# Forgetting attention and an MLP on one core: the shift as the exponential's bias, the start's decay rows re-cut, and unit 0's second layer in another order

## The chip, the core and the metric

The kernel runs on one core of a Trainium2 chip. A core has five engines with a queue each: PE (TensorE, matrix products), DVE (VectorE), ACT (ScalarE), POOL (GpSimd) and SP (SyncE, which here only issues DMAs). PE reads SBUF and writes PSUM; DVE and ACT read and write both; 16 DMA engines move data between HBM and SBUF. The metric is the device time of one execution in microseconds (us). The profile is one execution taken by the hardware profiler.

## The reference, cut to what matters

Inputs are q, k, v of shape (8 batches, 8 heads, 576 positions, 64) and f of shape (8, 8, 576), all float32, and two weights, 512 x 2048 and 2048 x 512.

```python
scores = scale * np.matmul(q, k.transpose(0, 1, 3, 2))          # scale = 1/8
log_f = np.log(np.clip(f, 0.0001, 1.0))
cum = np.cumsum(log_f, axis=-1)
decay = cum[:, :, :, None] - cum[:, :, None, :]
scores = np.where(causal, -1000000000.0, scores + decay)
attn = softmax(scores)                                          # written out, with + 1e-09 under the division
x = (attn @ v).transpose(0, 2, 1, 3).reshape(4608, 512)
h = x @ w_in
out = (h - np.tanh(h)) @ w_out
```

A term that is the same for all keys of one query leaves the softmax as it is: it multiplies numerator and denominator alike. The kernel uses this twice: a constant shift of 5 stands in place of the maximum, and the query's own decay need not be exact.

## The kernel before, in words

**Attention.** Work goes by pairs of heads, `pairs[p]` for p = 0 to 31, four pairs (`NPAIR`) in each of the eight batches. A score tile is computed transposed: keys on the partitions, queries along the columns. For one pair `TILES` lists seven score tiles (`ti` 0 to 6) of up to 512 columns. Each is a few matmuls into a PSUM tile `ps` (L358), one ACT exponential into an f16 tile `e` (or `el` for the tile of the last 64 keys, L367), and a causal mask: in batch 0 a matmul that adds -60000 through the tile `late` (L361), in the others a POOL select (L377). `values` multiplies `e` by `vn`, which holds v and a column of ones, into `av` (L395); DVE divides (L404 to L406) into `xn`; `turn` transposes `xn` into `XR`, the MLP's input, with PE and a copy in batch 0 (L423, L425, L427) and with two SP DMA transposes in the others (L429, L431).

**The decay inside the scores.** The matmul's contraction has 64 rows of the head and three more, kept in rows 64 to 66 of the tiles `QT` and `KT`. With the scale of 1/8 taken out, K's rows hold `chi` (8 cum, rounded to f16), `clo` (what the rounding left) and 1; q's rows hold -1, -1 and `cq` (8 cum - 40, f16). The product adds 8 (cum_q - cum_k) - 40 to 8 times the score, and the exponential's scale of 1/8 brings it back, with the shift of 5. The rows are moved into `QT` and `KT` by DMAs (`aug_rows`): on POOL for batch 0 (`bulk`, L219 to L221), on SP for the others (`load_aug`, L207).

**The first pair** does not wait for those DMAs. Its tiles are `QS` and `KS` (in the trace both are called W, since they lie in the weights' room), with 24 extra rows, three for each head of batch 0, at partitions 64 to 87 (`NH` to `NX`). `lf` holds f for 64 rows of all heads and again three times for batch 0's heads, so that `cum` has the values where they are wanted. For these rows `KS` gets -chi, 1 and the rest (L198), and q's row gets, for the head h in question alone, 1, 8 cum - 40 and -1 (`row_q`, L580, one ACT instruction for each head): q chooses the head. Per-partition factors for this lie in the columns of `per` (L179 to L191).

**The order.** All five engines run in the order in which the code issues (`manual_schedule`); nothing is reordered by a planner. At the start, DVE sets constants, clips f (L185), ACT takes Ln (L192) and loads the table for Exp (L193), DVE sums along the row (the scan, L195), makes chi (L197) and K's extra rows. `start` then issues pair 0: PE fills its time with matmuls on constants (`unread`, tile `idle`), transposes the raw q and k of the pair (L304), ACT copies q (L315), DVE copies k (L317) into `QS` and `KS` by head and half, and the first two score tiles follow. `bulk` issues the rest of batch 0's loads on POOL. From there `att_items(p)` gives the order within pair p: at given `ti` it puts the score tile, the transposes and copies of the next pair's q (`at_q`) and k (`at_k`), `values` of the pair before and `turn` of the one before that. The argument `copies` of `trans` names the engine of each copy, V for DVE and A for ACT.

**POOL's queue** issues the loads of q, k, v and the weights (they convert f32 to f16) in that same order, among the selects. `LOADS` says at which (p, ti); the first half of w_in is at (1, 0), the first of w_out at (4, 0).

**The MLP.** Its work goes by units of 512 tokens, woven into the attention from pair 4 on (`TAKE` is how many steps a pair gets). `mlp1` makes one of 16 blocks of 128 features: four matmuls into `hps` (L457), ACT's tanh into `th` (L462), DVE's sum into `gq` (L468). Features 0 to 7 are half 0 of `gq`, 8 to 15 are half 1. The second layer of unit 0 is `mlp2_plain`: 16 steps of eight matmuls each into `ops` (L498); four steps fill one PSUM bank, which holds two blocks of 128 tokens (`m`), each the sum over both halves of the features. The later units use `mlp2` (L523), which has seven products in place of eight.

Of the kernel before, what the change touches and what calls it, by code (L numbers as in the profile page):

```python
# [8 lines left out]
FP32 = mybir.dt.float32  # L9
FP16 = mybir.dt.float16  # L10
AF = mybir.ActivationFunctionType
# [5 lines left out]
SHIFT = 5.0  # L17
# [4 lines left out]
def kernel(  # L22
# [134 lines left out]
    nc.vector.memset(late, 0.0)  # L157
    nc.vector.memset(KT[0][:, :, S:PITCH], 0.0)
    chi = cst.tile([NX, S], FP16)
    clo = cst.tile([NH, S], FP16)  # L160
    cq = cst.tile([NH, S], FP16)
    KS = W1.rearrange("p k e -> p (k e)")[:, 0:2 * PITCH].rearrange("p (a n) -> p a n", a=2)
    QS = W2.rearrange("p k e -> p (k e)")[:, 0:2 * S].rearrange("p (a n) -> p a n", a=2)
    nc.vector.memset(KS[0:NX, :, S:PITCH], 0.0)
    per = cst.tile([NX, 9], FP32)
    nc.vector.memset(vn[0][D:P, NJ - 1, :, :], 0.0)
    isb, isc, mul_k, add_k, mul_l, mul_0, add_0, mul_1, add_1 = (per[:, i:i + 1] for i in range(9))
# [7 lines left out]
    def column(g, h):  # L175
        return id16[0:NX, NH + 3 * h + g:NH + 3 * h + g + 1]

    for to, g in ((isb, 1), (isc, 2)):
        nc.vector.tensor_reduce(out=to, in_=id16[0:NX, NH + g:NX:3], op=ALU.add, axis=mybir.AxisListType.X)  # L179
    nc.vector.tensor_scalar(out=mul_k, in0=isb, scalar1=-inv_qscale, scalar2=inv_qscale, op0=ALU.mult, op1=ALU.add)  # L180
    nc.vector.tensor_scalar_mul(out=add_k, in0=isb, scalar1=-1.0)
    nc.vector.tensor_scalar_mul(out=mul_l, in0=isc, scalar1=inv_qscale)
    for e in EL[0:2]:
        nc.vector.memset(e, 0.0)
    nc.vector.tensor_scalar(out=lf, in0=lf, scalar1=0.0001, scalar2=1.0,  # L185
                            op0=ALU.max, op1=ALU.min)
    nc.vector.memset(vn[0][:, :, :, D:VW], 1.0)
    for h, (mul, add) in enumerate(((mul_0, add_0), (mul_1, add_1))):
        nc.vector.tensor_scalar_mul(out=mul, in0=column(1, h), scalar1=inv_qscale)
        nc.vector.scalar_tensor_tensor(out=add, in0=mul, scalar=-SHIFT, in1=column(0, h), op0=ALU.mult, op1=ALU.add)  # L190
        nc.vector.tensor_tensor(out=add, in0=add, in1=column(2, h), op=ALU.subtract)  # L191
    nc.scalar.activation(out=lf, in_=lf, func=AF.Ln)  # L192
    nc.scalar.activation(out=expo, in_=lf[0:1, 0:1], func=AF.Exp)  # L193
    cum = TQ[0][0:NX, :, :].rearrange("p c s -> p (c s)").bitcast(FP32)[:, S:2 * S]
    nc.vector.tensor_tensor_scan(out=cum, data0=ones16, data1=lf, initial=0.0,  # L195
                                 op0=ALU.mult, op1=ALU.add)
    nc.vector.tensor_scalar(out=chi, in0=cum, scalar1=mul_k, scalar2=add_k, op0=ALU.mult, op1=ALU.add)  # L197
    nc.vector.scalar_tensor_tensor(out=KS[NH:NX, 0, 0:S], in0=cum[NH:NX, :], scalar=mul_l[NH:NX, :], in1=chi[NH:NX, :],  # L198
                                   op0=ALU.mult, op1=ALU.subtract)

    def aug_rows(b):
        i, hs = b % 2, slice(b * H, (b + 1) * H)
        return [(KT[i][D:D + 1, :, 0:S], chi[hs, :]), (KT[i][D + 1:D + 2, :, 0:S], clo[hs, :]), (QT[i][D + 2:D + 3, :, :], cq[hs, :])]

    def load_aug(b):
        for to, of in aug_rows(b):
# [6 lines left out]
    const_rows(0)  # L213

    def bulk():
        (k_hi, chi_0), (k_lo, clo_0), (q_hi, cq_0) = aug_rows(0)
        load_qk(qn, q, 0, 4, 6)
        load_qk(kn, k, 0, 4, 6)
        nc.gpsimd.dma_start(out=k_hi, in_=chi_0)  # L219
        nc.gpsimd.dma_start(out=q_hi, in_=cq_0)  # L220
        nc.gpsimd.dma_start(out=k_lo, in_=clo_0)  # L221
        load_qk(qn, q, 0, 6, H)
        load_qk(kn, k, 0, 6, H)
        for n in range(NJ - 1):
            load_v_block(0, n, 2, H)
# [117 lines left out]
    def scores(b, c, ti):  # L343
        if b == 0 and (((c - 1) * len(TILES) + ti) % 3 == 0 if c else ti == LAST):
            ps = ps_tr.tile([P, UW], FP32, tag="tr", name="ps")
        else:
            ps = ps_sc.tile([P, 512], FP32, tag="sc", name="ps")
        if ti == LAST:
            e = EL[(b * NPAIR + c) % 3]
        else:  # L350
            e = aex.tile([P, 512], FP16, tag="e", name="e")
        lo = min(x[4] for x in TILES[ti])
        hi = max(x[4] + x[3] for x in TILES[ti])
        kt, qt, rows = (KS, QS, NX) if b == 0 and c == 0 else (KT[b % 2], QT[b % 2], D + 3)
        for a, j, i0, n, col in TILES[ti]:
            h = 2 * c + a
            cut = min(P, n) if b == 0 and i0 == j * P else 0
            nc.tensor.matmul(out=ps[:, col:col + n], lhsT=kt[0:rows, h, j * P:(j + 1) * P],  # L358
                             rhs=qt[0:rows, h, i0:i0 + n], start=True, stop=cut == 0)
            if cut:  # L360
                nc.tensor.matmul(out=ps[:, col:col + cut], lhsT=id16, rhs=late[:, 0:cut],  # L361
                                 start=False, stop=True)
            for ib in range(j, NJ):
                w0 = min(ib * P, S - P)
                if i0 <= ib * P < i0 + n:
                    E[(b, c, a, j, ib)] = e[:, col + w0 - i0:col + w0 - i0 + P]
        nc.scalar.activation(out=e[:, lo:hi], in_=ps[:, lo:hi], func=AF.Exp, scale=qscale)  # L367
        if b == 0:
            return
        col, cp, step, wd = MASKS[ti]  # L370
        view = e[:, col:col + (cp - 1) * step + wd]
# [118 lines left out]
        nc.vector.tensor_tensor(out=LHS[name](u, i)[:, ks], in0=LHS[x](u, i)[:, ks], in1=LHS[y](u, i)[:, ks], op=op)  # L490

    def mlp2_plain(u, s):
        e, mp, m, half = s // 8, s // 4 % 2, s // 2 % 2, s % 2
        if s % 4 == 0:
            M2[u] = bank("ops").rearrange("p (m e) -> p m e", m=2)
        ops, t0 = M2[u], (2 * mp + m) * P
        for ft in range(half * NK, half * NK + NK):
            nc.tensor.matmul(out=ops[:, m, :], lhsT=GQ[(u, ft % NK // 4)][:, half, ft % 4, t0:t0 + P],  # L498
                             rhs=wout[:, ft, e * HE:(e + 1) * HE], start=(m == 0 and ft == 0),
                             stop=(m == 1 and ft == NFT - 1), skip_group_check=True)  # L500
# [75 lines left out]
    REST = []  # L576

    def start():
        def row_q(h, mul, add):
            nc.scalar.activation(out=QS[NH:NX, h, :], in_=cum[NH:NX, :], func=AF.Identity, bias=add[NH:NX, :], scale=mul[NH:NX, :])  # L580

        unread(47)
        row_q(0, mul_0, add_0)
        q_rest = trans(*pairs[0], qn, (QS,), True, "AAAA", True)
        nc.scalar.activation(out=cq, in_=cum[0:NH, :], func=AF.Copy, bias=-SHIFT * inv_qscale, scale=inv_qscale)
        unread(6)
        k_rest = trans(*pairs[0], kn, (KS,), True, "VVVV", True)
        unread(38)
        q_rest[0]()
        scores(*pairs[0], 0)  # L590
        unread(4)
        nc.vector.scalar_tensor_tensor(out=clo, in0=cum[0:NH, :], scalar=inv_qscale, in1=chi[0:NH, :], op0=ALU.mult, op1=ALU.subtract)
        nc.vector.tensor_copy(out=KS[NH:NX, 1, 0:S], in_=KS[NH:NX, 0, 0:S])
        for fn in k_rest:
            fn()
        scores(*pairs[0], 1)
        row_q(1, mul_1, add_1)
        unread(4)
        q_rest[1]()

    def last():
        nc.gpsimd.memset(KT[1][:, :, S:PITCH], 0.0)
# [4 lines left out]
    def att_items(p):  # L607
        def put(fn, *args):
            items.append((lambda: fn(*args), True))
# [6 lines left out]
        for ti in range(len(TILES)):  # L616
# [3 lines left out]
                items.append((lambda: const_rows(1), False))  # L620
                items.append((lambda: load_aug(1), False))
            if p == 0 and ti in (0, 2, 5, 6):
                put(unread, {0: 2, 2: 14, 5: 4, 6: 6}[ti])
            if p == 1 and ti == 6:
                put(unread, 8, True)
            if p == 1 and ti == 3:
# [100 lines left out]
```

## Time and profile before

| | us |
|---|---|
| median of 3 runs (341.08 to 341.85) | 341.27 |
| the profiled execution | 341.6 |
| its span | 339.9 |
| PE busy, of the span | 333.0 |
| DVE busy | 262.5 |
| ACT busy | 235.1 |
| POOL busy | 163.7 |
| first score of pair 0 | at 9.10 |
| first score of pair 1 | at 14.47 |
| first exponential of pair 2 | at 19.07 |
| first matmul of `mlp1` | at 28.91 |
| first matmul of `mlp2_plain` | at 50.75 |

Times inside the execution count from the start of the span. A row of the timeline reads: start, duration, engine, line, operation, output<-input, shapes, how many, and in brackets the idle time ahead of it and who ended it. PEld is PE's loading of the stationary operand, which overlaps its matmuls; rows with a q behind the engine's name (SPq) are DMAs being issued, and a transfer lands some microseconds later. A busy PE can be one that waits inside a group of matmuls, so the starts of the matmuls tell more than the share.

### The profile page before, as it was taken

The page shows a single profiled execution, that of the slowest core. Times are in us where ns is not written, and L with a number is a line of the kernel's source. Part 1 is how long each engine was busy: PE and PEld are TensorE (multiplying, and loading weights), DVE is VectorE, ACT ScalarE, POOL GpSimd, SP SyncE. Part 2 cuts the span into 40 slices and gives each one's busy share as a digit, 9 for nine tenths or more (in the row PEclk, how much of TensorE's full clock was granted, in tenths as well). Part 3 has the DMA queues.
Part 4 walks back from the last instruction along what each step waited for, and adds up shares of the span by engine and source line. Part 5 has one row for each costly group of instructions (what it writes and reads, how often), then busy time and mean ns, then how long its engine had stood idle before and what let it go on. Part 6 is the DMA issues. An engine that isn't in the chain of part 4 may idle for free.

```text
span 339.9 us, 8804 instructions
## 1 busy us (share of the span) xinstructions
PE 333.0 (98%) x3345; PEld 237.7 (70%) x3345; DVE 262.5 (77%) x516; ACT 235.1 (69%) x440; POOL 163.7 (48%) x323
## 2 busy tenths in 40 slices
PE   8999999999999999999999999999999999999995
PEld 8775557875588558855788888656875686486485
DVE  8898986659888888678967886688668766966864
ACT  6998777878987886778677867787558743632630
POOL 8894765885657573677377647632322210000000
PEclk9999999999999999999999999999999999999999
DMA  9999999999959999999999999990130023002003
GB/s 116 124 173 201 187 198 179 153 162 196 137 93 181 159 116 92 136 168 130 106 106 191 131 110 112 165 133 15 49 115 13 17 62 101 0 31 95 1 16 109
DMA packets 147535, 38.88 MB, mean 114 GB/s; under 512 B 128221, under 2 KB 146381, under 8 KB 147493
## 3 DMA queue, kind: packets, MB, share of 16 engines
q0 software_dynamic: 94592, 18.39, 74.1%
q1 hardware_dynamic: 52868, 19.88, 31.7%
q8 instruction: 26, 0.43, 0.5%
q14 instruction: 17, 0.13, 0.2%
q10 hardware_dynamic: 32, 0.06, 0.0%
HBM read 36.90 MB, written 9.44 MB: 136 GB/s over the span
## 4 chain that ended last, share of the span: by engine, by line
PE 85%; DVE 8%; DMA 2%; ACT 2%; issue 1%; ACTq 0%
PE hps L457 35%; PE ops L523 29%; PE ps L358 11%; PE av L395 7%; DMA XR<-xn 2%; PE ops L498 2%; DVE KT L317 2%; DVE QT L317 1%; ACT e L367 1%; DVE gq L468 1%; PE t L304 1%; DVE xn L406 1%; DVE W L317 1%; PE x L423 0%; DVE TQ L195 0%
## 5 line engine op out<-in xcount | busy, mean ns | idle before, releaser
L457 PE MATMUL hps<-XR,win 128*128 128x512 f16 (+1 forms) x640 | 140.9, 357 | 0.5 <-DMA XR<-xn 0.3
L462 ACT ACTIVATE th<-hps 128x512 f32<-128x512 f32 x144 | 86.6, 602 | 55.5 <-PE hps L457 52.8
L367 ACT ACTIVATE e<-ps 128x512 f16<-128x512 f32 x192 | 110.5, 598 | 9.8 <-PE ps L358 7.9
L468 DVE TENSOR_TENSOR gq<-hps,th 128x512 f16<-128x512 f32 x144 | 98.1, 687 | 24.2 <-ACT th L462 22.6
L377 POOL TENSOR_SCALAR_AFFINE_SELECT e<-e 128x128 f16<-128x128 f16 x168 | 60.3, 362 | 69.9 <-ACT e L367 67.9
L457 PEld LDWEIGHTS <-win 128*128 128x128 f16 x640 | 57.7, 97 | 48.7 <-issue 0.7
L358 PE MATMUL ps<-QT,KT 67*128 67x512 f16 (+1 forms) x372 | 73.8, 277 | 0.8 <-ACT e L367 0.4
L523 PEld LDWEIGHTS <-gq 128*128 128x128 f16 x640 | 60.2, 97 | 11.2
L523 PE MATMUL ops<-wout,gq 128*128 128x256 f16 x512 | 63.2, 272 | 0.0
L358 PEld LDWEIGHTS <-KT 67*128 67x128 f16 x372 | 35.3, 98 | 22.2 <-issue 1.2
L395 PEld LDWEIGHTS <-e 128*128 128x128 f16 x896 | 32.3, 97 | 3.6
L395 PE MATMUL av<-vn,e 128*128 128x65 f16 x896 | 33.6, 193 | 0.0
L131 POOL DMA_DIRECT2D vn<-in_v_dram x32 | 28.0, 878 | 7.5 <-DMA win<-in_moe_w_in_dram 3.4
L523 PE MATMUL ops<-W,sq 128*128 128x256 f16 x256 | 31.2, 272 | 0.0
L406 DVE TENSOR_TENSOR xn<-av,rs 128x640 f16<-128x640 f32 x32 | 26.4, 825 | 1.1
L523 PEld LDWEIGHTS <-sq 128*128 128x128 f16 x256 | 24.1, 97 | 3.4
L108 POOL DMA_DIRECT2D qn<-in_q_dram x25 | 21.1, 845 | 3.7 <-DMA wout<-in_moe_w_out_dram 1.9
L377 POOL TENSOR_SCALAR_AFFINE_SELECT el<-el 128x128 f16<-128x128 f16 x28 | 9.4, 337 | 26.9 <-ACT el L367 26.7
L108 POOL DMA_DIRECT2D kn<-in_k_dram x25 | 21.1, 845 | 1.5 <-issue 1.1
L404 DVE TENSOR_SCALAR rs<-av 128x10 f32<-128x10 f32 x32 | 5.2, 162 | 18.1 <-PE av L395 17.0
L498 PE MATMUL ops<-wout,gq 128*128 128x256 f16 x128 | 16.9, 272 | 0.4 <-DVE gq L468 0.3
L317 DVE COPY QT<-t 64x576 f16<-64x576 f16 x18 | 14.4, 801 | 3.5 <-PE t L304 3.4
(93 smaller groups left out, 321.0 us busy)
## 6 DMA issues: line engine op xcount, KB each, us to landing
out_dram<-ost SPq DMA_DIRECT2D x34, 256.0 KB
vn<-in_v_dram POOLq DMA_DIRECT2D x24, 128.0 KB, 5.6
qn<-in_q_dram POOLq DMA_DIRECT2D x20, 128.0 KB, 4.9
kn<-in_k_dram POOLq DMA_DIRECT2D x20, 128.0 KB, 5.0
win<-in_moe_w_in_dram POOLq DMA_DIRECT2D x2, 1024.0 KB, 12.3
wout<-in_moe_w_out_dram POOLq DMA_DIRECT2D x2, 1024.0 KB, 17.0
XR<-xn SPq DMA_TRANSPOSE x56
qn<-in_q_dram POOLq DMA_DIRECT2D x6, 144.0 KB, 4.7
```

Source lines behind the costliest of these rows:

```text
L108: nc.gpsimd.dma_start(out=dst[b % 2][0:pn, n, :].rearrange("p (h d) -> p h d", h=H), in_=src[b, :, n * P:n * P + pn, :].rearrange("h p d - ...
L131: nc.gpsimd.dma_start(out=vn[b % 2][:, n, h0:h1, 0:D], in_=v[b, h0:h1, n * P:(n + 1) * P, :].rearrange("h p d -> p h d"))
L317: nc.vector.tensor_copy(out=to, in_=of)
L358: nc.tensor.matmul(out=ps[:, col:col + n], lhsT=kt[0:rows, h, j * P:(j + 1) * P], rhs=qt[0:rows, h, i0:i0 + n], start=True, stop=cut == 0)
L367: nc.scalar.activation(out=e[:, lo:hi], in_=ps[:, lo:hi], func=AF.Exp, scale=qscale)
L377: nc.gpsimd.affine_select(out=view, in_=view, compare_op=ALU.is_ge, fill=0.0, base=0, pattern=pat, channel_multiplier=-1)
L395: nc.tensor.matmul(out=av[:, a, ib, :], lhsT=E.pop((b, c, a, j, ib)), rhs=vn[b % 2][:, j, 2 * c + a, 0:D + 1], start=(j == 0), stop=(j == ib))
L406: nc.vector.tensor_tensor(out=xn.rearrange("p i (a d) -> p a i d", a=2), in0=av[:, :, :, 0:D], in1=rs.to_broadcast([P, 2, NJ, D]), op=ALU. ...
L457: nc.tensor.matmul(out=hps[:, o:o + n], lhsT=win[:, ci, ft * P:(ft + 1) * P], rhs=XR[:, ci, t:t + n], start=(ci == 0), stop=(ci == NCH - 1))
L462: nc.scalar.activation(out=th, in_=hps, func=AF.Tanh, scale=-1.0)
L468: nc.vector.tensor_tensor(out=GQ[(u, i)][:, half, kt, :], in0=hps, in1=th, op=ALU.add)
L523: nc.tensor.matmul(out=ps[:, m, :], lhsT=LHS[lhs](u, kt // 4)[:, kt % 4, m * P:(m + 1) * P], rhs=rhs[:, kt, :], start=(fresh and (apart or ...
```

## The change

1. The shift of 5 is no longer part of the decay rows. A tile `shift` of 128x1 holds -5 and is the exponential's bias.
2. With that, q's decay row is 8 cum, which is chi; `cq` and its ACT instruction (L585) go, and `aug_rows` sends chi to q as well as to k.
3. In the first pair the head is chosen in K's rows. q's extra rows are made once for all heads (one ACT instruction instead of two) and copied to head 1 by DVE; `clo` is made for all 88 rows in one DVE instruction, and `row_k(h, of)` multiplies its rows 64 to 87 by a 0-or-1 column for head h, for head 0 ahead of `start`, for head 1 behind the first score tile. The separate `clo` (L592) and the copy of K's rows (L593) go. The factors in `per` are made by two reductions and fewer instructions.
4. The clip, Ln and the scan are done in two halves of 288 columns.
5. All four q copies of pair 0 are issued ahead of the first score; of the two copies of pair 1's k, one is moved from DVE to ACT (`copies` "AV" where it was "VV").
6. POOL's three DMAs of decay rows move ahead of the loads of heads 4 and 5.
7. Fill matmuls: 38 become 32 ahead of the first score, 14 become 4 after tile 2.
8. In `mlp2_plain` the two loops over `half` and `m` change places: both token blocks on half 0, and then both on half 1.

```diff
-    clo = cst.tile([NH, S], FP16)
-    cq = cst.tile([NH, S], FP16)
+    clo = cst.tile([NX, S], FP16)
+    shift = cst.tile([P, 1], FP32)
+    nc.vector.memset(shift, -SHIFT)
...
-    for to, g in ((isb, 1), (isc, 2)):
-        nc.vector.tensor_reduce(out=to, in_=id16[0:NX, NH + g:NX:3], op=ALU.add, axis=mybir.AxisListType.X)
+    nc.vector.tensor_reduce(out=per[:, 0:3], in_=id16[0:NX, NH:NX].rearrange("p (h g) -> p g h", g=3),
+                            op=ALU.add, axis=mybir.AxisListType.X)
+    nc.vector.tensor_reduce(out=per[:, 8:10], in_=id16[0:NX, NH:NH + 6].rearrange("p (h g) -> p h g", g=3),
+                            op=ALU.add, axis=mybir.AxisListType.X)
...
+    nc.vector.memset(mul_l[0:NH, :], inv_qscale)
...
-    nc.vector.tensor_scalar(out=lf, in0=lf, scalar1=0.0001, scalar2=1.0,
-                            op0=ALU.max, op1=ALU.min)
+    cum = TQ[0][0:NX, :, :].rearrange("p c s -> p (c s)").bitcast(FP32)[:, S:2 * S]
+    PART = [slice(0, S // 2), slice(S // 2, S)]
+    for n in PART:
+        nc.vector.tensor_scalar(out=lf[:, n], in0=lf[:, n], scalar1=0.0001, scalar2=1.0, op0=ALU.max, op1=ALU.min)
+        nc.scalar.activation(out=lf[:, n], in_=lf[:, n], func=AF.Ln)
+    nc.scalar.activation(out=expo, in_=lf[0:1, 0:1], func=AF.Exp)
+    nc.vector.tensor_scalar_mul(out=mul_q, in0=isb, scalar1=inv_qscale)
+    nc.vector.tensor_tensor(out=add_q, in0=isa, in1=isc, op=ALU.subtract)
     nc.vector.memset(vn[0][:, :, :, D:VW], 1.0)
-    for h, (mul, add) in enumerate(((mul_0, add_0), (mul_1, add_1))):
-        nc.vector.tensor_scalar_mul(out=mul, in0=column(1, h), scalar1=inv_qscale)
-        nc.vector.scalar_tensor_tensor(out=add, in0=mul, scalar=-SHIFT, in1=column(0, h), op0=ALU.mult, op1=ALU.add)
-        nc.vector.tensor_tensor(out=add, in0=add, in1=column(2, h), op=ALU.subtract)
-    nc.scalar.activation(out=lf, in_=lf, func=AF.Ln)
-    nc.scalar.activation(out=expo, in_=lf[0:1, 0:1], func=AF.Exp)
-    cum = TQ[0][0:NX, :, :].rearrange("p c s -> p (c s)").bitcast(FP32)[:, S:2 * S]
-    nc.vector.tensor_tensor_scan(out=cum, data0=ones16, data1=lf, initial=0.0,
-                                 op0=ALU.mult, op1=ALU.add)
+    for i, n in enumerate(PART):
+        nc.vector.tensor_tensor_scan(out=cum[:, n], data0=ones16[:, n], data1=lf[:, n],
+                                     initial=cum[:, n.start - 1:n.start] if i else 0.0, op0=ALU.mult, op1=ALU.add)
     nc.vector.tensor_scalar(out=chi, in0=cum, scalar1=mul_k, scalar2=add_k, op0=ALU.mult, op1=ALU.add)
-    nc.vector.scalar_tensor_tensor(out=KS[NH:NX, 0, 0:S], in0=cum[NH:NX, :], scalar=mul_l[NH:NX, :], in1=chi[NH:NX, :],
-                                   op0=ALU.mult, op1=ALU.subtract)
+    nc.vector.scalar_tensor_tensor(out=clo, in0=cum, scalar=mul_l, in1=chi, op0=ALU.mult, op1=ALU.subtract)
+
+    def row_k(h, of):
+        nc.vector.tensor_scalar_mul(out=KS[NH:NX, h, 0:S], in0=clo[NH:NX, :], scalar1=of[NH:NX, :])
+
+    row_k(0, of_0)
...
-        (k_hi, chi_0), (k_lo, clo_0), (q_hi, cq_0) = aug_rows(0)
+        (k_hi, chi_0), (k_lo, clo_0), (q_hi, _) = aug_rows(0)
+        nc.gpsimd.dma_start(out=k_hi, in_=chi_0)
+        nc.gpsimd.dma_start(out=q_hi, in_=chi_0)
+        nc.gpsimd.dma_start(out=k_lo, in_=clo_0)
         load_qk(qn, q, 0, 4, 6)
         load_qk(kn, k, 0, 4, 6)
-        nc.gpsimd.dma_start(out=k_hi, in_=chi_0)
-        nc.gpsimd.dma_start(out=q_hi, in_=cq_0)
-        nc.gpsimd.dma_start(out=k_lo, in_=clo_0)
...
-        nc.scalar.activation(out=e[:, lo:hi], in_=ps[:, lo:hi], func=AF.Exp, scale=qscale)
+        nc.scalar.activation(out=e[:, lo:hi], in_=ps[:, lo:hi], func=AF.Exp, bias=shift, scale=qscale)
...
     def mlp2_plain(u, s):
-        e, mp, m, half = s // 8, s // 4 % 2, s // 2 % 2, s % 2
+        e, mp, half, m = s // 8, s // 4 % 2, s // 2 % 2, s % 2
...
     def start():
-        def row_q(h, mul, add):
-            nc.scalar.activation(out=QS[NH:NX, h, :], in_=cum[NH:NX, :], func=AF.Identity, bias=add[NH:NX, :], scale=mul[NH:NX, :])
-
         unread(47)
-        row_q(0, mul_0, add_0)
+        nc.scalar.activation(out=QS[NH:NX, 0, :], in_=cum[NH:NX, :], func=AF.Identity, bias=add_q[NH:NX, :], scale=mul_q[NH:NX, :])
         q_rest = trans(*pairs[0], qn, (QS,), True, "AAAA", True)
-        nc.scalar.activation(out=cq, in_=cum[0:NH, :], func=AF.Copy, bias=-SHIFT * inv_qscale, scale=inv_qscale)
+        for fn in q_rest:
+            fn()
         unread(6)
         k_rest = trans(*pairs[0], kn, (KS,), True, "VVVV", True)
-        unread(38)
-        q_rest[0]()
+        unread(32)
         scores(*pairs[0], 0)
         unread(4)
-        nc.vector.scalar_tensor_tensor(out=clo, in0=cum[0:NH, :], scalar=inv_qscale, in1=chi[0:NH, :], op0=ALU.mult, op1=ALU.subtract)
-        nc.vector.tensor_copy(out=KS[NH:NX, 1, 0:S], in_=KS[NH:NX, 0, 0:S])
+        row_k(1, of_1)
+        nc.vector.tensor_copy(out=QS[NH:NX, 1, :], in_=QS[NH:NX, 0, :])
         for fn in k_rest:
             fn()
         scores(*pairs[0], 1)
-        row_q(1, mul_1, add_1)
         unread(4)
-        q_rest[1]()
...
-                put(unread, {0: 2, 2: 14, 5: 4, 6: 6}[ti])
+                put(unread, {0: 2, 2: 4, 5: 4, 6: 6}[ti])
...
-                put(trans, *after, kn, KT, early, "AV" if early and p > 1 else "VV")
+                put(trans, *after, kn, KT, early, "AV" if early and p != 1 else "VV")
```

More of the change, by code (lines that the diff above doesn't have):

```diff
@@ L164 @@
     nc.vector.memset(KS[0:NX, :, S:PITCH], 0.0)
-    per = cst.tile([NX, 9], FP32)
+    per = cst.tile([NX, 10], FP32)
     nc.vector.memset(vn[0][D:P, NJ - 1, :, :], 0.0)
-    isb, isc, mul_k, add_k, mul_l, mul_0, add_0, mul_1, add_1 = (per[:, i:i + 1] for i in range(9))
+    isa, isb, isc, mul_k, add_k, mul_l, mul_q, add_q, of_0, of_1 = (per[:, i:i + 1] for i in range(10))
     EL = [cst.tile([P, 192], FP16, tag=f"el{i}", name=f"el{i}") for i in range(3)]
@@ L173 @@
                             base=0, pattern=[[1, P]], channel_multiplier=-1)
-    def column(g, h):
-        return id16[0:NX, NH + 3 * h + g:NH + 3 * h + g + 1]
-    for to, g in ((isb, 1), (isc, 2)):
-        nc.vector.tensor_reduce(out=to, in_=id16[0:NX, NH + g:NX:3], op=ALU.add, axis=mybir.AxisListType.X)
+    nc.vector.tensor_reduce(out=per[:, 0:3], in_=id16[0:NX, NH:NX].rearrange("p (h g) -> p g h", g=3),
+                            op=ALU.add, axis=mybir.AxisListType.X)
+    nc.vector.tensor_reduce(out=per[:, 8:10], in_=id16[0:NX, NH:NH + 6].rearrange("p (h g) -> p h g", g=3),
+                            op=ALU.add, axis=mybir.AxisListType.X)
     nc.vector.tensor_scalar(out=mul_k, in0=isb, scalar1=-inv_qscale, scalar2=inv_qscale, op0=ALU.mult, op1=ALU.add)
@@ L201, in aug_rows @@
+    row_k(0, of_0)
     def aug_rows(b):
         i, hs = b % 2, slice(b * H, (b + 1) * H)
-        return [(KT[i][D:D + 1, :, 0:S], chi[hs, :]), (KT[i][D + 1:D + 2, :, 0:S], clo[hs, :]), (QT[i][D + 2:D + 3, :, :], cq[hs, :])]
+        return [(KT[i][D:D + 1, :, 0:S], chi[hs, :]), (KT[i][D + 1:D + 2, :, 0:S], clo[hs, :]), (QT[i][D + 2:D + 3, :, :], chi[hs, :])]
     def load_aug(b):
```

## The prediction

> **What bounds the kernel now.** I read the page first, then the stages, then the chain of work that ended last, then the rows where that chain changes engine. The profiled execution spans 339.9 us and took 341.6 us, 1.7 us of it outside the span and 0.33 us above the median of 341.27. I forecast differences and take them from the median. About 0.2% (0.7 us) is what a measurement here can tell from no change.
>
> ```profile
> PE 333.0 (98%) x3345; PEld 237.7 (70%) x3345; DVE 262.5 (77%) x516; ACT 235.1 (69%) x440; POOL 163.7 (48%) x323
> ...
> PE 85%; DVE 8%; DMA 2%; ACT 2%; issue 1%; ACTq 0%
> ```
> ```profile
> 9.00:14.00 5.00, 4.63 (x64) 3.76 (x65) 4.84 (x9) 4.86 (x10) 4.41 (x7) 1.00 0.95 128
> ...
> 50.00:55.00 5.00, 4.49 (x38) 2.95 (x36) 4.25 (x8) 2.94 (x6) 2.83 (x7) 1.00 1.43 199
> ...
> 80.00:150.00 70.00, 70.00 (x684) 47.93 (x683) 57.31 (x115) 54.51 (x105) 44.19 (x85) 1.00 1.44 140
> 150.00:250.00 100.00, 100.00 (x1035) 75.06 (x1034) 77.17 (x157) 73.78 (x143) 53.19 (x112) 1.00 1.17 114
> ```
>
> In the stages (columns: busy PE, PEld, DVE, ACT, POOL, clock, DMA share, GB/s) PE is full from 80 us on, so whatever arrives there earlier ends earlier. All that the change touches lies before 70 us, and there the chain is not PE's:
>
> ```profile
> 5.25 1.28 DVE TQ L195
> 6.55 0.66 DVE chi L197
> 7.24 0.81 DVE W L198
> ...
> 8.57 0.48 DVE W L317
> 9.08 0.76 DVE clo L592
> 9.86 0.30 DVE W L593
> ...
> 13.61 0.82 DVE KT L317
> 14.47 0.39 PE ps L358
> ```
>
> The chain is DVE without a gap from 1.2 us to the second pair's first score at 14.47. Later it leaves DVE for PE at 53.86, and at 67.83 it goes through one DMA:
>
> ```profile
> 52.61 1.20 DVE gq L468 x2
> 53.81 0.05 issue
> 53.86 0.28 PE ops L498
> ...
> 66.98 0.82 DVE xn L406
> 67.81 0.03 DVE W L284
> 67.83 7.57 DMA XR<-xn
> 75.40 0.04 issue
> 75.45 0.38 PE hps L457
> ```
>
> **The change, part by part.** *The bias of the exponential.* 192 ACT rows read another constant tile in place of the zero one; the form is the same (512 columns, 598 ns), so nothing. Its memset, and one more for `mul_l`, go ahead of the clip, where small DVE instructions start 0.07 us apart (3.37, 3.44, 3.50): +0.15, clip at 3.92 instead of 3.77.
>
> *Ln and scan by halves.* ACT exponentials of 128 and 512 columns (274 and 596 ns) give 0.84 ns per column and 0.17 fixed, so half of Ln is 0.41. The clip is 0.46 whole; I take 0.30 for a half, the scan's half (1.35 whole) 0.75. First half: clip to 4.22, Ln to 4.68. Second: clip to 4.50, Ln to 5.09. Scans 4.74 to 5.49 and 5.52 to 6.27; before, the scan ended at 6.52. The six column instructions at 4.24 to 5.24 that held the scan until 5.17 become two, under Ln. Gain 0.25; bounds 0 (fixed costs of the halves doubled) and 0.45. The table load for Exp follows Ln 0.15 later and ends 6.4; with the small Exp behind it, ACT is free at 6.6, and q's row (0.86) plus four copies (0.49) end at 9.4, before the first score is read: covered.
>
> *Head chosen in K's rows.* chi 0.65 and a three-input row of 88x576 (0.81, as the 24x576 one) stay; `row_k` is added: 24x576 f16 to f16 with a scalar per row. Nearest rows: the copy of the same shape and types, 0.30, and chi, the same operation from f32 with two operations, 0.65. I take 0.30, since types and size are the copy's; 0.65 stays as a bound. In the Trainium skill, "VectorE: DVE Perf Modes", section "The perf-mode tier table", copy and tensor_scalar on 16-bit SBUF data share the fourfold rate; by that it is 0.30, by chi's row the sum below would lose 0.7. With 0.03 between instructions: scan 6.27, chi 6.95, clo 7.79, row 8.12, two copies (0.48) 9.11. Before they ended at 9.05: the first score is 0.06 later.
>
> *After the first score.* Leaving DVE: clo, 0.76. Staying in other form: 0.30 for head 1's K rows; added: 0.30 copying q's row to head 1. Two K copies then end at 10.76 (before 11.14). Pair 1's QT copies end at 12.4, and of its two KT copies only one (0.81) is DVE's: 13.2 against 14.43. ACT loses two rows of 0.86 and 0.68 (before: the second `row_q` at 10.72, cq at 8.43), moves the last q copies ahead of the exponentials and takes one KT copy of 0.82. From a first exponential at 9.67 it has six tiles of 0.57, one of 0.28 and the copy: pair 1 begins at 14.15 (before 14.96), pair 2 at 17.87. DVE gives the same: transposes after pair 1's first score, four copies of 0.81, pair 2's score at 17.3 and its exponential at 17.8. Before it began at 19.07. **Gain 1.2**; bounds 0.5 (both K rows at 0.65) and 1.4 (scan at its best). From there ACT is dense until 26.8 before and after. The 16 fill matmuls taken out (0.057 each) cover the waits that go.
>
> *POOL's queue.* Before: q and k of heads 4 and 5 at 6.79, then a wait of 0.78 for cq and 0.19 before clo. After: three aug rows of 0.57, 0.53 and 0.51 at 6.98 to 8.6, with no wait, since chi is done at 6.95 and clo at 7.79; then those two loads at 8.6 and 9.25, landing by 13.4 and 14.1 (4.8 as before), needed at 13.8 and 14.2: covered, barely. The v blocks start at 11.15 instead of 11.90, so this queue gains 0.75. The first half of win, issued 17.68 and landed 28.28, was used at 28.91; now it lands at 27.53 and is wanted at 27.71: covered. SP's rows for the next batch wait for chi and clo alone and only gain.
>
> *Halves of unit 0.* The second step of `mlp2_plain` starts at 52.36 on features whose last two activations DVE finishes at 53.2 and 53.81. Its eight matmuls of 0.109 would end at 53.23 and end at 53.97. Now it reads half 0, ready by then; half 1 comes in the third step, 53.72 by the earlier start, whose eighth matmul (54.5) is past 53.81. ACT waits 1.50 for PE there, so no exponential holds PE. **Gain 0.7**; bounds 0 and 0.74.
>
> *The transposes behind it.* PE stalls 0.27 at 75.45 for XR. They are issued when xn is ready, so with equal latency (7.57) issue and need move together: 0. Bounds: +0.27, and minus all of the gain if the landing stays where it is.
>
> Sum: 1.2 + 0.7 = 1.9, so 339.7 for this execution, 339.4 from the median.
>
> **The rivals.** *A, the DMA holds the gain.* Loads issued from 18 to 70 us land 6 to 22 us later, at some 200 GB/s up to 55 us: the stream is full, and moves by POOL's 0.75 only. If XR lands by that, at 74.65, the gain is 0.75: 340.5. For it: the full stream. Against: the transposes are in SP's queue, not behind POOL's loads. *B, one of the two parts pays little:* K's rows at 0.65 (0.5 + 0.7), or the third step meets another wait (1.2 + 0): 340.1. For the first speaks chi's row; against the second ACT's idle 1.50. *C, slower:* PE reaches the XR wait 1.9 earlier while the backlog, moved by 0.75 only, is 1.15 us deeper for it, and the transposes take longer. It decides from a latency of 9.5 (7.57 + 1.9). With the 10.4 of the load issued at 57.39 the end is 0.9 later: 342.2. For it: those loads' 10 to 11 us; against it: those issued at 64.83 to 67.21 land within 6.7, and 1.15 us is the distance of one load. By the Trainium skill, "DMA: Bandwidth & Descriptors", section "Queues, rings and completion order", an engine takes turns between queues packet by packet, so a deeper POOL backlog would not delay SP's; that speaks against A and C, and no run yet shows it. *D, nothing:* the start is used up at win's landing and the halves at XR's: 341.2.
>
> **How the numbers follow.** The likeliest, both parts paid in full: 0.47, own range 338.9 to 339.9. B 0.16, A 0.15, D 0.05, C 0.17. Faster: the likeliest, B and half of A, whose 340.5 lies at the bound: 0.70. Same: the rest of A and D: 0.13. Slower: C, 0.17. The range leaves out C and what is under 338.9 (the sum with the upper bounds, 2.4): 338.9 to 341.2.
>
> **What would show it.** Right: the scan's end near 6.3, K's row at 0.30, pair 1's first score near 13.25, pair 2's exponentials near 17.9, the second `ops` step without a wait for gq and 1.9 us earlier at its end, the XR wait still about 0.3. Wrong: a K row at 0.65, PE waiting for win at 28 or for XR by more than 1 us, or transposes of q for pair 2 held by their load.

## The result: 1.3% slower, and the profile after

The changed kernel takes 345.87 us, median of four runs (345.85 to 345.90), where the kernel before took 341.18 (341.08 to 341.85; a fourth run beside the three of the table above). The ratio is 1.0133, with a 95% interval of 1.0116 to 1.0151. The forecast was 339.4, with a range that ended at 341.2. The profiled execution after took 345.9 us and spans 344.2, so it stands for the median as it is.

From the page of the profile after: the busy time of each engine, the chain that ended last by engine, and the groups of the exponential, the tanh and the score matmuls (busy us and mean ns of one, then idle time ahead of it and what ended most of it):

```profile
PE 334.4 (97%) x3329; PEld 237.1 (69%) x3329; DVE 259.9 (76%) x516; ACT 249.4 (72%) x440; POOL 167.4 (49%) x323
...
PE 83%; ACT 9%; DVE 5%; issue 2%; ACTq 0%; DVEq 0%
...
L372 ACT ACTIVATE e<-ps,shift 128x512 f16<-128x512 f32 x192 | 127.1, 689 | 7.7 <-PE ps L363 5.0
L467 ACT ACTIVATE th<-hps 128x512 f32<-128x512 f32 x144 | 87.1, 606 | 50.7 <-PE hps L462 49.4
...
L363 PE MATMUL ps<-QT,KT 67*128 67x512 f16 (+1 forms) x372 | 75.5, 276 | 2.7 <-ACT e L372 2.3
```

Before, one exponential took 598 ns, ACT was busy for 235.1 us and had 2% of the chain. Now an exponential takes 689 ns, ACT is busy 14.3 us longer and has 9% of the chain. The tanh beside it did not change (602 before, 606 now), so ACT itself is no slower: one kind of instruction is. Score matmuls waited 0.4 us for ACT before; now 2.3.

The same stages as before (columns: busy PE, PEld, DVE, ACT, POOL with their counts, clock, DMA share, GB/s):

```profile
9.00:14.00 5.00, 3.81 (x51) 2.94 (x52) 4.29 (x8) 4.27 (x9) 5.00 (x9) 1.00 0.82 105
50.00:55.00 5.00, 4.80 (x43) 3.24 (x42) 4.89 (x10) 3.56 (x6) 3.99 (x9) 1.00 1.44 199
80.00:150.00 70.00, 69.12 (x676) 47.19 (x674) 54.52 (x112) 56.67 (x102) 44.06 (x83) 1.00 1.31 134
150.00:250.00 100.00, 99.54 (x1011) 72.85 (x1010) 75.62 (x154) 78.15 (x142) 55.31 (x111) 1.00 1.15 113
```

From 150 to 250 us PE's busy time fell from 100.00 to only 99.54, but it ran 1011 matmuls in place of 1035, and ACT's busy time rose from 73.78 to 78.15. PE's busy share says little here on how fast it gets on; where the work stands at a given time does. For that I compare when DVE starts the division `xn` of each pair, in the two profiled executions:

| pair | before, us | after, us | later by |
|---|---|---|---|
| 0 | 18.95 | 19.16 | 0.21 |
| 5 | 51.78 | 53.01 | 1.23 |
| 6 | 58.25 | 58.74 | 0.49 |
| 12 | 110.91 | 112.52 | 1.61 |
| 16 | 146.28 | 148.67 | 2.39 |
| 24 | 217.28 | 221.11 | 3.83 |
| 31 | 277.88 | 282.16 | 4.28 |

The loss grows over the whole attention, with some steps back, the largest of 0.74 between pairs 5 and 6, where the exchanged loops lie. After the last pair nothing more is lost (the spans differ by 4.3). One stretch, pair 11's end to pair 12, shows how it comes about. ACT's timeline before (start, duration, line, operation, shapes, count):

```profile
104.05 0.60 ACT L367 ACTIVATE e<-ps 128x512 f16<-128x512 f32 x1 [0.17 <-PE ps L358]
104.67 0.68 ACT L118 ACTIVATE QT<-TQ 64x576 f16<-64x576 f16 x1
...
106.45 0.57 ACT L367 ACTIVATE e<-ps 128x512 f16<-128x512 f32 x1
107.05 0.68 ACT L118 ACTIVATE QT<-TQ 64x576 f16<-64x576 f16 x1
107.64 1.70 ACT L367 ACTIVATE e<-ps 128x512 f16<-128x512 f32 x3
```

ACT's timeline after:

```profile
105.15 0.69 ACT L372 ACTIVATE e<-ps,shift 128x512 f16<-128x512 f32 x1 [0.22 <-PE ps L363]
105.86 0.68 ACT L118 ACTIVATE QT<-TQ 64x576 f16<-64x576 f16 x1
...
107.73 0.67 ACT L372 ACTIVATE e<-ps,shift 128x512 f16<-128x512 f32 x1
108.42 0.68 ACT L118 ACTIVATE QT<-TQ 64x576 f16<-64x576 f16 x1
109.13 1.90 ACT L372 ACTIVATE e<-ps,shift 128x512 f16<-128x512 f32 x3
```

From the first of these exponentials to the group of three, ACT needs 3.59 us before and 3.98 after. Before, ACT here is already no faster than PE (a score tile and eight matmuls take about 1.1 us, an exponential and a copy 1.2); the two PSUM buffers for score tiles are just enough to hide it. After, they are not, and the chain of work that ended last passes through ACT there:

```profile
104.84 0.23 PE ps L363
...
105.15 0.69 ACT e L372
105.84 0.03 issue
105.86 0.34 ACT QT L118
106.20 0.37 issue
106.57 0.70 ACT e L372
...
107.31 0.39 PE ps L363
```

Before, the chain from 104 to 110 us is PE alone. From pair 11 to pair 12 the kernel falls 0.52 further behind (1.09 to 1.61). That the number of buffers sets the limit is read from these chains; no run changed it.

At the start the chain after reads:

```profile
5.73 0.83 DVE TQ L196
6.58 0.58 DVE chi L198
7.19 0.82 DVE clo L199
8.04 0.36 DVE W L202
...
9.44 0.39 PE ps L363
...
12.52 0.69 ACT KT L320
13.21 0.54 ACT e L372
13.79 0.30 PE ps L363
...
14.68 0.38 PE ps L363
```

The first score is at 9.44 (before 9.10), and pair 1's first score at 14.68 (before 14.47): the shortened start is no shorter. What led to pair 1 was DVE's copies before; now it is the copy that went to ACT, with an exponential queued behind it and a score tile behind that.

At the exchanged loops, and where PE waited for XR before:

```profile
53.39 0.38 PE ps L363
53.76 0.88 PE ops L503 x8
...
75.42 0.86 PE hps L462 x4
```

The second step of eight `ops` matmuls no longer waits for `gq`, and the 7.57 us DMA has left the chain.

### The profile page after: what moved, and what is told of

Same layout as the page of the kernel before. It is cut to its first block, busy times and chain, and to the rows that moved or that the text cites. A ratio compares the mean times of both kernels' runs of the same rounds, so it can differ in the third digit from the quotient of the medians.

```text
span 344.2 us, 8770 instructions
## 1 busy us (share of the span) xinstructions
PE 334.4 (97%) x3329; PEld 237.1 (69%) x3329; DVE 259.9 (76%) x516; ACT 249.4 (72%) x440; POOL 167.4 (49%) x323
## 3 DMA queue, kind: packets, MB, share of 16 engines
HBM read 36.90 MB, written 9.44 MB: 135 GB/s over the span
## 4 chain that ended last, share of the span: by engine, by line
PE 83%; ACT 9%; DVE 5%; issue 2%; ACTq 0%; DVEq 0%
PE hps L462 35%; PE ops L528 23%; PE ps L363 12%; PE av L400 8%; ACT e L372 6%; PE ops L503 3%; ACT QT L118 2%; PE t L309 1%; ACT th L467 1%; DVE gq L473 1%; DVE QT L322 0%; DVE KT L322 0%; DVE TQ L196 0%; ACT KT L320 0%; PE x L428 0%
## 5 line engine op out<-in xcount | busy, mean ns | idle before, releaser
L372 ACT ACTIVATE e<-ps,shift 128x512 f16<-128x512 f32 x192 | 127.1, 689 | 7.7 <-PE ps L363 5.0
L382 POOL TENSOR_SCALAR_AFFINE_SELECT e<-e 128x128 f16<-128x128 f16 x168 | 64.3, 386 | 76.0 <-ACT e L372 75.2
L363 PE MATMUL ps<-QT,KT 67*128 67x512 f16 (+1 forms) x372 | 75.5, 276 | 2.7 <-ACT e L372 2.3
L528 PE MATMUL ops<-wout,gq 128*128 128x256 f16 x512 | 63.2, 272 | 0.0
L372 ACT ACTIVATE el<-ps,shift 128x128 f16<-128x128 f32 x32 | 11.7, 364 | 9.3 <-PE ps L363 9.2
```

Source lines behind the costliest of these rows:

```text
L528: nc.tensor.matmul(out=ps[:, m, :], lhsT=LHS[lhs](u, kt // 4)[:, kt % 4, m * P:(m + 1) * P], rhs=rhs[:, kt, :], start=(fresh and (apart or ...
```

## The experiments

The main theory, P: a scale or bias that lies in a 128x1 tile makes an ACT instruction 0.09 us longer than one given as a number, and ACT is too near PE's pace to hide that. Its rival, S: the re-cut start or the new order of queues and loops lost the time, and the longer exponential is off the path. Each run is compared with runs of the kernel before on the same chip, whose medians lie between 341.21 and 341.26.

**The bias alone.** The kernel before, with a tile of zeros as the exponential's bias; nothing else.

```diff
+    shift = cst.tile([P, 1], FP32)
+    nc.vector.memset(shift, 0.0)
-        nc.scalar.activation(out=e[:, lo:hi], in_=ps[:, lo:hi], func=AF.Exp, scale=qscale)
+        nc.scalar.activation(out=e[:, lo:hi], in_=ps[:, lo:hi], func=AF.Exp, bias=shift, scale=qscale)
```

> The kernel before with one thing added: a 128x1 tile of zeros as the bias of every exponential (its value changes nothing). Theory P (the pointer operand): each of the 192 exponentials takes about 0.09 us longer, 689 ns instead of 598 for 512 columns, and where ACT alternates an exponential and a tanh behind PE's steps it falls behind: 346.5 us, between 345 and 348. Rival S (the re-cut start is the loss, or the added waits of the first pairs): the tile is just another constant, and this stays at 341.2 to 342.

Measured: 346.61 (346.47 to 346.81) against 341.23, ratio 1.0156 [1.0142 to 1.0170]: 5.4 us. From its page, the chain by engine, the exponential and the score matmuls:

```profile
PE 82%; ACT 10%; DVE 5%; issue 2%; ACTq 0%
...
L369 ACT ACTIVATE e<-ps,shift 128x512 f16<-128x512 f32 x192 | 127.1, 690 | 7.9 <-PE ps L360 5.8
...
L360 PE MATMUL ps<-QT,KT 67*128 67x512 f16 (+1 forms) x372 | 75.5, 276 | 2.7 <-ACT e L369 2.3
```

The same rows as in the changed kernel, and the `xn` of the last pair 5.22 later than before. P holds and S falls: this one operand costs more than the whole change lost.

**The scale from a tile**, the bias left a number:

```diff
+    sc8 = cst.tile([P, 1], FP32)
+    nc.vector.memset(sc8, qscale)
-        nc.scalar.activation(out=e[:, lo:hi], in_=ps[:, lo:hi], func=AF.Exp, scale=qscale)
+        nc.scalar.activation(out=e[:, lo:hi], in_=ps[:, lo:hi], func=AF.Exp, scale=sc8)
```

> The kernel before with the exponential's scale of 1/8 from a 128x1 tile instead of a number. If any pointer operand costs the 0.09 us, this is the run with the bias tile again: 689 ns for 512 columns and 346.6 us. If only the bias has that price: 598 ns and 341.2.

Measured: 346.64 (two runs) against 341.26, ratio 1.0153 [1.0136 to 1.0171], 689 ns for an exponential. It is the operand that costs, not what is added or multiplied.

**A bias tile for the 144 tanh** instead:

```diff
+    nil = cst.tile([P, 1], FP32)
+    nc.vector.memset(nil, 0.0)
-        nc.scalar.activation(out=th, in_=hps, func=AF.Tanh, scale=-1.0)
+        nc.scalar.activation(out=th, in_=hps, func=AF.Tanh, bias=nil, scale=-1.0)
```

> The kernel before with a tile of zeros as the bias of the 144 tanh in place of the 192 exponentials. If the loss comes where ACT has to put an exponential and a tanh behind each of PE's steps, the tanh are as good a place to lose it, less where exponentials stand without tanh (the MLP's second layer): 343.5 us, between 342.5 and 345.5, and nothing lost behind the last pair. If it is the exponentials' own chain to the two score buffers alone: 341.2 to 342.

Measured: 343.01 (two runs) against 341.26, ratio 1.0047 [1.0029 to 1.0065], 1.75 us; a tanh takes 696 ns (602 before). The same 0.09 on 144 instructions costs a third of what it costs on 224 (192 exponentials of 512 columns and 32 of 128). The last `xn` is 1.58 later, and the MLP behind it loses next to nothing more: the tanh cost time only beside the attention.

**The change without the bias, first form.** The shift goes back into q's decay row, so `cq` and its ACT instruction come back; all else is the change.

```diff
-    shift = cst.tile([P, 1], FP32)
-    nc.vector.memset(shift, -SHIFT)
+    cq = cst.tile([NH, S], FP16)
...
+    nc.vector.scalar_tensor_tensor(out=add_q, in0=mul_q, scalar=-SHIFT, in1=add_q, op0=ALU.mult, op1=ALU.add)
...
-        nc.scalar.activation(out=e[:, lo:hi], in_=ps[:, lo:hi], func=AF.Exp, bias=shift, scale=qscale)
+        nc.scalar.activation(out=e[:, lo:hi], in_=ps[:, lo:hi], func=AF.Exp, scale=qscale)
...
         q_rest = trans(*pairs[0], qn, (QS,), True, "AAAA", True)
+        nc.scalar.activation(out=cq, in_=cum[0:NH, :], func=AF.Copy, bias=-SHIFT * inv_qscale, scale=inv_qscale)
```

> The changed kernel with the shift back in q's rows, as before (cq made by ACT between the copies of head 0 and head 1, minus 40 in the first pair's factor), and the exponential without a bias tile; all else of the change stays. Theory P: 0.37 us from the start (pair 2's first exponential near 18.7 instead of 19.07) and 0.74 from unit 0's loops: 340.1 us, between 339.4 and 340.6. Rival S: the start still loses what it lost: 343 to 345.

Measured: 341.71 (340.67 to 343.54) against 341.23, ratio 1.0010 [0.9995 to 1.0026]. The loss is gone, but the gain that was left over, 340.1 by the expectation, did not show in the median. In the profiled execution, a short one of 340.73, POOL's queue waits 1.60 us for `cq`, whose DMA now stands ahead of the big loads; what the longer executions lost was not profiled.

**The same with the old order of the loops in `mlp2_plain`:**

```diff
-        e, mp, half, m = s // 8, s // 4 % 2, s // 2 % 2, s % 2
+        e, mp, m, half = s // 8, s // 4 % 2, s // 2 % 2, s % 2
```

> As the run with the shift back in the rows, but with unit 0's loops as before: the start's re-cut alone. Theory P: 0.1 to 0.6 us faster than before, 340.8 us. Rival S: 343 to 346.

Measured: 341.43 (341.39 to 342.4), ratio 1.0006 [0.9997 to 1.0015]. By `xn` the start is 0.10 behind at pair 0 and 0.38 at pairs 2 to 8; then the wait for XR is gone and it is level (-0.05 at pair 9). The new start is worth nothing that shows in this form.

**The loops alone**, in the kernel before:

```diff
-        e, mp, m, half = s // 8, s // 4 % 2, s // 2 % 2, s % 2
+        e, mp, half, m = s // 8, s // 4 % 2, s // 2 % 2, s % 2
```

> The kernel before with only the two loops of unit 0's second layer exchanged. The prediction's step: the wait for the last two activations at 53.2 and 53.8 goes, 0.74 us, and the rest moves along: 340.5 us, between 340.3 and 340.8. Rival A (the transposes behind it hold the gain): 341.0 to 341.3, with the wait for XR grown from 0.3 to about 1 us.

Measured: 341.25 (340.99 to 341.91) against 341.23, ratio 0.9998 [0.9989 to 1.0007]: no gain. In its profiled execution `xn` of pairs 6 to 8 is 0.78 earlier, and then the chain goes through the transpose:

```profile
66.20 0.82 DVE xn L406
67.03 0.03 DVE W L284
67.06 7.79 DMA XR<-xn
74.85 0.04 issue
74.89 0.38 PE hps L457
```

Issued 0.77 earlier (67.06 against 67.83), it took 7.79 instead of 7.57 and landed 0.55 earlier. Up to there the loops gave what was forecast of them, and the DMA kept a part. Why the median shows nothing of the rest stays open: this profiled execution (340.99) is the shortest of its eleven, and that of the kernel before (341.6) lies above its median.

**The change without the bias, second form.** The shift is a 68th row of the contraction, -1 in q times 40 in K, so nothing waits for `cq`. The row of 40 is made by a POOL memset.

```diff
+    forty = TK[0:H, 2, :]
+    nc.gpsimd.memset(forty, SHIFT * inv_qscale)
...
-        nc.sync.dma_start(out=QT[i][D:D + 2, :, :], in_=minus16)
-        nc.sync.dma_start(out=KT[i][D + 2:D + 3, :, 0:S], in_=ones16[0:H, :])
+        nc.sync.dma_start(out=QT[i][D:D + 3, :, :], in_=minus16)
+        nc.sync.dma_start(out=KT[i][D + 3:D + 4, :, 0:S], in_=ones16[0:H, :])
+        nc.sync.dma_start(out=KT[i][D + 2:D + 3, :, 0:S], in_=forty)
...
-        nc.scalar.activation(out=e[:, lo:hi], in_=ps[:, lo:hi], func=AF.Exp, bias=shift, scale=qscale)
+        nc.scalar.activation(out=e[:, lo:hi], in_=ps[:, lo:hi], func=AF.Exp, scale=qscale)
```

> The changed kernel without the bias tile, the shift carried by a constant: one more contraction row, -1 in q's tile against 40 in k's (two more small DMAs of constants, one POOL memset in POOL's wait for chi), and -40 in the first pair's factor. q's row stays chi, POOL's queue does not wait for ACT. Theory P (the pointer operand was the loss): 340.4 us, between 340.0 and 341.0, and less spread than the run with cq on ACT, in which POOL waited 1.6 us for it. Rival A (loads and transposes hold what is gained): 341.0 to 341.7, as the run with cq.

Measured: 340.79 (340.69 to 342.96) against 341.26, ratio 0.9988 [0.9976 to 1.0000], so a gain of 0.5 us at the edge of what can be told from none. **The same with the old loops** (the edit shown above):

> As the run with the constant row, with unit 0's loops as before: the re-cut start alone, without the wait for cq. The prediction's step (1.2 us from the start): 340.0. After the rows of the changed kernel (scan no earlier, K's row at 0.36, the ACT copy of pair 1's k ahead of the DVE copy and not beside it): 341.0, between 340.7 and 341.5.

Measured: 341.53 (341.45 to 343.74), ratio 1.0008 [0.9995 to 1.0022]. Between the two the loops are worth 0.74, all the way to the end: in this kernel PE does not wait for XR, so their gain stays. The new start alone is 0.3 us slower than the old one in the median, which its interval does not tell from no difference. By the ratios of the two kernels with and without the bias (1.0133 and 0.9988), the bias costs the changed kernel about 5 us (the second form also has the row of 40).

The next four take the start apart. **The row of 40 by ACT**, in the second form:

```diff
-    nc.gpsimd.memset(forty, SHIFT * inv_qscale)
+    nc.scalar.activation(out=forty, in_=ones16[0:H, :], func=AF.Copy, scale=SHIFT * inv_qscale)
```

> As the run with the constant row, with the row of 40 made by ACT in its wait for the clip instead of by POOL: chi, which took 0.93 us beside POOL's memset there, should take 0.57 to 0.65 again, and the chain of the start, which runs through it, should be 0.3 shorter: first score near 9.45 instead of 9.77, 340.5 us in all, between 340.2 and 340.9. If the start does not reach the end: 340.8, as that run.

Measured: 341.46 (340.56 to 343.05) against 341.21, ratio 1.0010 [0.9997 to 1.0023]; the profiled execution is one of the short ones, 340.64. The first score is at 9.42 where it was at 9.77, so the DVE side gained 0.35, and the time did not. POOL's timeline of this kernel:

```profile
8.47 0.51 POOL L227 DMA_DIRECT2D KT<-clo  x1
8.97 0.66 POOL L102 DMA_DIRECT2D qn<-in_q_dram  x1
9.62 0.67 POOL L102 DMA_DIRECT2D kn<-in_k_dram  x1
11.29 0.63 POOL L102 DMA_DIRECT2D qn<-in_q_dram  x1 [0.99 <-DMA vn<-in_v_dram]
12.47 0.63 POOL L102 DMA_DIRECT2D kn<-in_k_dram  x1 [0.55 <-DMA vn<-in_v_dram]
13.25 3.32 POOL L131 DMA_DIRECT2D vn<-in_v_dram  x4
```

By the trace's releasers the queue stands until earlier loads of v have landed; the v blocks start at 13.25 (before 11.90), and PE then waits 0.3 us for one of them. The order of the queue alone does not bring this about. In the changed kernel, which has the same order, the queue did not stand and the v blocks started at 11.53: the three v loads of 64 KB ahead landed 4.9 us after their issue there, 7.3 here (medians). The two further kernels below that keep this order and ACT's row stood 1.35 and 1.51 us in their profiled executions. What made those landings late is not shown.

**The loads of heads 4 and 5 first**, as before the change, then the decay rows:

```diff
+        load_qk(qn, q, 0, 4, 6)
+        load_qk(kn, k, 0, 4, 6)
         nc.gpsimd.dma_start(out=k_hi, in_=chi_0)
         nc.gpsimd.dma_start(out=q_hi, in_=chi_0)
         nc.gpsimd.dma_start(out=k_lo, in_=clo_0)
-        load_qk(qn, q, 0, 4, 6)
-        load_qk(kn, k, 0, 4, 6)
```

> As the run with ACT's row of 40, with the loads of heads 4 and 5 ahead of the decay rows in POOL's queue as before. The prediction's step (POOL's queue moves 0.75 earlier by the other order): the first half of win is issued later by 0.3 to 0.7 here, and if the gain of unit 0's loops needs that room, part of it goes: 340.6 to 341.2. If the queue's order does not matter: as that run, with less spread at the transposes of pair 2.

Measured: 340.46 (340.24 to 341.43) against 341.21, ratio 0.9979 [0.9971 to 0.9988]. POOL's timeline:

```profile
6.62 0.70 POOL L102 DMA_DIRECT2D qn<-in_q_dram  x1
7.28 0.68 POOL L102 DMA_DIRECT2D kn<-in_k_dram  x1
...
9.63 0.51 POOL L229 DMA_DIRECT2D KT<-clo  x1 [0.53 <-DVE W L325]
...
11.79 3.35 POOL L131 DMA_DIRECT2D vn<-in_v_dram  x4
```

This one move is worth 1.0 us in the median (341.46 to 340.46, on the same chip), and the runs lie closer together. It beats both kernels: 0.75 us under the one before, 5.4 under the changed one. In the two profiled executions the difference is only 0.4 and appears at pair 2 (`xn` 27.32 against 26.94); what the longer executions of the other order lose beyond that was not profiled. The expectation had this order no faster, with `win` issued 0.3 to 0.7 later; it was issued 1.40 earlier (17.64 against 19.04).

**The clip, Ln and scan whole again:**

```diff
-    for n in PART:
-        nc.vector.tensor_scalar(out=lf[:, n], in0=lf[:, n], scalar1=0.0001, scalar2=1.0, op0=ALU.max, op1=ALU.min)
-        nc.scalar.activation(out=lf[:, n], in_=lf[:, n], func=AF.Ln)
+    nc.vector.tensor_scalar(out=lf, in0=lf, scalar1=0.0001, scalar2=1.0, op0=ALU.max, op1=ALU.min)
+    nc.scalar.activation(out=lf, in_=lf, func=AF.Ln)
...
-    for i, n in enumerate(PART):
-        nc.vector.tensor_tensor_scan(out=cum[:, n], data0=ones16[:, n], data1=lf[:, n],
-                                     initial=cum[:, n.start - 1:n.start] if i else 0.0, op0=ALU.mult, op1=ALU.add)
+    nc.vector.tensor_tensor_scan(out=cum, data0=ones16, data1=lf, initial=0.0, op0=ALU.mult, op1=ALU.add)
```

> As the run with ACT's row of 40, with clip, Ln and scan whole instead of in halves. The prediction's step (halves end the scan 0.25 earlier): 0.25 slower than that run. After the rows of the changed kernel, where the halved scan takes 1.68 us instead of 1.35 and ends at 6.55: the scan ends at 6.5 either way, no difference beyond 0.1.

Measured: 341.07 (340.41 to 342.93), ratio 0.9993 [0.9981 to 1.0005]. The scan ends at 6.61 (5.26 + 1.35) where the halves ended at 6.53 (4.92 + 1.61), and the first score comes at 9.51 against 9.42. The halves are worth 0.08 us at that place; the medians cannot tell.

**Both K copies of pair 1 on DVE again** ("VV" for it):

```diff
-                put(trans, *after, kn, KT, early, "AV" if early and p != 1 else "VV")
+                put(trans, *after, kn, KT, early, "AV" if early and p > 1 else "VV")
```

> As the run with ACT's row of 40, with both copies of pair 1's k on DVE as before. The prediction's step (the two engines copy beside each other): 0.8 later at pair 1's first score. After the rows of the changed kernel, where DVE's copy waits for ACT's (0.39 us, both write one tile): 0.2 earlier to 0.3 later, and ACT freed of 0.81 us; end within 0.3 of that run.

Measured: 341.42 (340.31 to 343.34), ratio 1.0003 [0.9990 to 1.0016]. Pair 1's first score is at 14.53, against 14.57 with one copy on ACT: no difference. With ACT's help, DVE's copy waits 0.39 us for ACT's and they run one after the other.

## Why the prediction was wrong

**The step that failed** is the first: "192 ACT rows read another constant tile in place of the zero one; the form is the same (512 columns, 598 ns), so nothing." No exponential read a zero tile: the trace of before has the memset of one (`const-float32-0.0`, POOL at 0.31 us) and no reader of it. A tile as bias or scale is one operand more than a number, and it costs 689 - 598 = 91 ns on 512 columns and 364 - 275 = 89 ns on 128. The form of the output is the same, the list of inputs isn't (`e<-ps` became `e<-ps,shift`). The price stood in the trace of before, in two neighbouring groups of ACT with the same 576 columns, one with scale and bias from the tile `per` (function Identity), one with numbers (Copy):

```profile
L580 ACT ACTIVATE W<-TQ,per 24x576 f16<-24x576 f32 x2 | 1.7, 860 | 0.1
L585 ACT ACTIVATE cq<-TQ 64x576 f16<-64x576 f32 x1 | 0.7, 683 | 0.0
```

Their 177 ns for two operands are 0.09 each, and 224 exponentials would be, by this estimate, 20 us more on ACT, which the forecast should have set against a chain in which ACT had 2%. (In the run with the bias alone ACT's busy time rose by 15.1 us, 235.1 to 250.2, less than the estimate; in a run of three in a row each cost only 0.07 more.) In the Trainium skill, "ScalarE: Activation LUTs", section "What ACT_TABLE_LOAD costs", each 128x1 pointer operand is said to add about 93 ns to an ACTIVATE; the 91 measured here agree. That ACT was idle for 31% of the span did not cover it. The exponential is one of two links between score tiles, and with two PSUM buffers it needs to keep up with PE in every stretch, not on average; with the bias alone 5.4 us came out.

**None of the rivals held this cause.** The slower one, C, was a late XR. XR was not late in the changed kernel: its wait is gone.

**The halves of unit 0: right**, in mechanism and size. The step back of 0.74 after pair 5, 0.78 in the loops alone and 0.74 between the two kernels with 68 rows answer to the 0.7 forecast.

**The transposes behind it: mixed.** The forecast's "with equal latency (7.57) issue and need move together: 0" failed both ways. In the loops alone the latency grew by 0.22, PE's wait went from 0.27 to 0.50, and the median showed no gain. The outcome is that of rival A, but the DMA itself is seen to take only 0.22 of the 0.78, and that the full stream of loads is the reason is not shown. In the kernels with the new start PE reaches XR without a wait, which is worth 0.4 (the `xn` of pair 9 against pair 8: -0.73 against -0.30 in the second form). In the kernel with the loads first, XR landed within 7.2 us of its issue (issued at 67.20; the fourth matmul of the step, the one that waited before, starts at 74.37). That the DMAs' load at that time made the difference is likely; it is not shown.

**The start: wrong, 0 in place of 1.2.** By its terms, in the changed kernel:

- Clip and Ln as forecast: two clips 0.66 (0.60), two Ln 0.78 together (0.82). A half of the scan takes 0.84, not 0.75, and its end came at 6.55, not 6.27, where the kernel before had 6.52: no gain. Against the whole scan in the kernel with ACT's row of 40, the gain of 0.25 measured 0.08.
- K's row: 0.36, not 0.30; the first score at 9.44, not 9.16. The row to take was neither the copy nor chi, but it lay much nearer the copy; the equal rate that the prediction took for the two was 0.06 off.
- After the first score, the 1.2: pair 1's first score came at 14.68, not 13.25. The forecast added DVE's and ACT's copies as if side by side. They ran in turn, and ACT's copy stood between exponentials, so that PE's own next tile waited for ACT until 13.79. With the copy back on DVE, DVE's four copies in a row bring it to 14.53, so either way ends at about the same time. Pair 2's first score came at 18.73 (before 18.53), so nothing of the 1.2 was left there.
- POOL's queue: "gains 0.75" measured 0.37 in the changed kernel (v blocks at 11.53 against 11.90), a loss of 1.35 in the kernel with ACT's row of 40, and undoing this move alone made that kernel 1.0 us faster. The step counted only what POOL waits for at DVE and ACT, not that the queue can also stand until its earlier loads have landed.

Without the bias, then, the forecast's sum of 1.9 came to about 0.5 in the second form (340.79 against 341.26), and to 0.75 with the loads in their old place: 0.7 from the loops, up to 0.4 from the XR wait in the profiled executions, and nothing or a small loss from the start. The profiled execution of before held the XR wait and lay 0.3 above its median, so differences of profiles (338.6 against 339.9 us of span) show more than the medians do.

## What to carry to other kernels

Read the inputs of a group, not only its shape: an operand that moves from a number to a tile changes the price of every instance, and the trace often holds both forms side by side. Multiply such a difference by the count and set it against the engine that paces each stretch, not against its mean share: an engine at 69%, as ACT was here behind two buffers, can have no room at all, and a PE busy for 99.5% can be one that waits. Where a copy moves to a second engine, ask whether the two copies can overlap and what is queued behind it there; where small DMAs move ahead of large ones, ask when the queue next has to wait for a landing.

## What the runs showed of the hardware

- A scale or a bias from a 128x1 tile lengthens an ACT instruction by 0.09 us, whether it is the exponential (598 to 689 ns), the tanh (602 to 696) or 128 columns (275 to 364). In a run of three in a row it was 0.07 each (1.70 to 1.90).
- The same DVE instruction, chi, took 0.93 us in the kernel whose row of 40 is made by POOL, and 0.57 in the one where ACT makes it. DVE's timeline in the first, and then in the second:

```profile
6.56 0.93 DVE L200 TENSOR_SCALAR chi<-TQ,per 88x576 f16<-88x576 f32 x1
```

```profile
6.56 0.57 DVE L200 TENSOR_SCALAR chi<-TQ,per 88x576 f16<-88x576 f32 x1
```

  It starts at the same time in both, and the one edit between them moves the row of 40 from POOL's memset (6.61 to 7.18) to ACT; the first score came 0.35 us later beside the memset.
- POOL's queue of loads can stand until an earlier load has landed, by the trace's releasers, though no engine's instruction holds it: 0.99 and 0.55 us for the loads of v at the start, and 3.2 us for `win` later, in the kernel with ACT's row of 40. In the changed kernel it did not stand for the loads of v.
